# Tail tokens of two batches in one pass of the channel layers, with new work orders, in an attention and MLP-mixer kernel

## The chip, the cores and the metric

The kernel runs on one core of a Trainium2 chip. The metric is the device time of one execution in microseconds, as a median over several executions. Details come from one execution that was taken with the hardware profiler. All times are in microseconds (us) unless marked ns.

## The reference

What is computed is sliding-window attention with a distance bias for 8 batches, 8 heads, 576 tokens and head dimension 64, and then one mixer layer on its output x (576 tokens x 512 channels for each batch).

```python
scores = scale * np.matmul(q, k.transpose(0, 1, 3, 2))
rel = pos[:, None] - pos[None, :]
bias = slopes[:, None, None] * (-np.abs(rel))[None]
mask = (rel >= 0) & (rel < 128)
attn = softmax(np.where(mask, scores + bias[None], -1e9))
x = (attn @ v) with heads side by side          # 8 x 576 x 512

h = np.maximum(x^T @ w_tok1, 0.0) @ w_tok2      # over tokens: 576 -> 256 -> 576
u = x + h^T
h2 = np.maximum(u @ w_ch1, 0.0) @ w_ch2         # over channels: 512 -> 1536 -> 512
return u + h2
```

## The kernel before

The matrices are held in bf16, sums in fp32. A batch has 576 tokens: four blocks of 128 and a tail of 64. Everything that works on blocks of 128 tokens has a part of its own for the tail.

The work of a batch is cut into named steps, and the order in which they are issued is written out by hand as lists of names. A name without a mark is the current batch b; one mark means b+1, two b+2, three b+3. PROLOGUE and FIRST cover batch 0 and the start, SECOND batch 1, PERIOD is run for b = 2 to 6, LAST is batch 7. Each engine executes its own instructions strictly in the order of the list. The steps that matter here:

- S..: scores of one key block and four heads, on TensorE into one of two double banks psS, then an exp on ScalarE and a mask multiply on VectorE. The mask multiply is issued one step later than its scores (MASK_LATER). These matmuls contract over 64 rows.
- P0 to P3, P4: the product with V, also into psS; VectorE divides by the row sum (L382, L383; for the tail L408, L413) and so frees psS.
- K0, K1: the first token layer. U0 to U3: the second token layer and the add of x, giving the tile ub. UT: the same for the 64 tail tokens, which gives the transposed tile utt directly (psT, copied by ScalarE, L474).
- X0 to X3: transposes of ub into utb, which the channel layer reads. For batches 3 to 7 (U_DMA) the step is a DMA transpose of two blocks, issued from SyncE; for batches 1 and 2 it is a TensorE transpose and a copy, on VectorE for the blocks in X_DVE and on ScalarE for others. Batch 0 has its own forms u0 to u3 and x0 to x3, by pairs of heads; for a u in U_ACT the residual goes in by identity matmuls and ScalarE copies the result, for others VectorE adds it (L667, L669).
- C0 to C11: the first channel layer, one step for each of 12 blocks of 128 hidden channels: four matmuls of 512 columns into one of three banks psM, then a relu on VectorE (for the blocks in DVE_RELU, L504) or on ScalarE (L507). The three psM banks go round among C, D, E, K, U and X.
- T0, T1: the first channel layer for the 64 tail tokens of one batch: six hidden blocks each, 24 matmuls of 64 columns into the one bank psT, then one relu of ScalarE of 384 columns (L516, L519).
- D00 to D32: the second channel layer for the four token blocks, each in three parts of four matmuls, with an add of ub on VectorE and an output DMA at the end (L549 to L555).
- E0 to E2: the second channel layer for the tail. The tails of batches b-1 and b (b odd) make one block of 128 tokens, so E exists for odd b alone. After its 12 matmuls four identity matmuls of 128 columns add the transposed utt (L575), ScalarE copies the sum out (L579), and two output DMAs follow (L581).
- Lq, Lk, v: loads from GpSimd's queue. Zq, Zk: DMA transposes of queries and keys from SyncE's queue (L213, L216), which also takes all output DMAs. The loads of the next keys wait until Zk has read the previous ones.

Of the kernel before, what the change touches and what calls it, by code (L numbers as in the profile page):

```python
# [11 lines left out]
ALU = mybir.AluOpType  # L12
# [4 lines left out]
CH2_PARTS = 3  # L17
MASK_LATER = 1
U_DMA = (3, 4, 5, 6, 7)
U_ACT = (0, 1, 3)  # L20
X_DVE = (0, 1, 2)
K_DVE = (0,)
PROLOGUE = """
l0 I W2 q0 q1 J M3 l1 ck0 M0 W3 M1 W3 W3 l23 cq0 O qt m0 A0 q23 W3 v3 v0 ck1 v1 M2 FC W1 cq1 A1
# [1 line left out]
l23' A1' e1 qt' W2 v4' ek p2 u0 A0' p3 G1 k2 S00' LC G2 u1 v1'  # L26
"""
FIRST = """
H1 v3' k3 u2 v2' x0 u3 A3' v0' W1 H0 A2' Lk'' UT x2 x1 AT' Lq'' S20' x3 Zq'' Zk'' Lk''' T0 S10'
S01' v3'' v0'' Lq''' C9 v0''' S21' C11 v4'' C3 e2 S31' C0 C5 S30' C7 C8 S11' C10 E0 C1 C2 v2''  # L30
C4 P2' v4''' C6 P3' D00 P0' P4' T1 E2 v1'' P1' D01 D02 K0' K1' D10 U1' v2''' D11 D12 U2' UT'
Zq''' X1' U0' U3' D20 D30 S11'' S20'' v1''' D21 D31 E1 Zk''' S00'' D22 S01'' D32
"""
SECOND = """
T1 X2 X0 X3 S30' S31' T0 C8 C9 C7 C11 C2 P0' C5 Lk''' C3 v0''' C4 v1''' C1 S21' S10' C10 Lq'''
v2''' v3'' C0 P4' C6 D00 P3' D01 v3''' P1' P2' D02 K0' S20'' K1' v4''' S01'' D10 D11 D12 U1' U0'
UT' U2' U3' X0' S21'' S11'' D20 D21 X3' S10'' S00'' E0 E1 D22 E2 X2' D30 D31 X1' D32 P0''
# [12 lines left out]
SPLIT = (1, 2)  # L50
S_M = (0, 2, 4, 5, 6)
S_P = ()
x_DVE = (1, 2, 3)
k_DVE = (2,)
AK_DVE = (2, 3, 7)
AQ_ACT = (1, 3, 4, 5, 7)
DVE_RELU = (2, 3, 4, 5, 7, 8, 10, 11)


@with_exitstack  # L60
def kernel(
# [11 lines left out]
    nc = tc.nc  # L73
    P = nc.NUM_PARTITIONS
# [8 lines left out]
    ST = S - SM  # L83
    NHP = H // 2
    NHT = DCH // P
    NCB = DM // P
# [15 lines left out]
    psT = PS("psT", [P, 512])  # L102
# [15 lines left out]
    ident = T("ident", [P, P])  # L118
# [36 lines left out]
    utt = [T(f"utt{i}", [P, NCB, 2, ST]) for i in range(2)]  # L155
    r2 = [T(f"r2_{i}", [P, NHT, SM]) for i in range(2)]
    r2t = [T(f"r2t{i}", [P, NHT, 2, ST]) for i in range(2)]
    ob = [T(f"ob{i}", [P, DM], f32) for i in range(4)]
    orot = [0]

# [128 lines left out]
    def score(b, kb, j):  # L289
# [188 lines left out]
    def utrans(b, c):  # L478
# [9 lines left out]
        def f():  # L488
            t = M()[:, 0:256].bitcast(bf16)
            for cb in range(NCB):  # L490
                nc.tensor.transpose(t[:, cb * P:(cb + 1) * P],  # L491
                                    ub[b % 2][:, c, cb * P:(cb + 1) * P], ident[:, :])
            cp = nc.vector.tensor_copy if c in X_DVE else nc.scalar.copy
            cp(out=utb[b % 2][:, c, :, :], in_=t.rearrange("p (g x) -> p g x", g=NCB))
        return f

    def ch1(b, ht):
        def f():
            t = M()
            for cb in range(NCB):  # L500
                nc.tensor.matmul(t[:, :], lhsT=WC1[:, cb, ht * P:(ht + 1) * P],  # L501
                                 rhs=utb[b % 2][:, :, cb, :], start=(cb == 0), stop=(cb == NCB - 1))
            if ht in DVE_RELU:
                nc.vector.tensor_scalar(out=r2[b % 2][:, ht, :], in0=t[:, :], scalar1=0.0,  # L504
                                        scalar2=None, op0=ALU.max)
            else:
                nc.scalar.activation(out=r2[b % 2][:, ht, :], in_=t[:, :], func=ACT.Relu)  # L507
        return f

    def ch1_tail(b, g, n=6):  # L510
        def f():
            for j in range(n):
                ht = g * n + j
                o = psT[:, j * ST:(j + 1) * ST]
                for cb in range(NCB):
                    nc.tensor.matmul(o, lhsT=WC1[:, cb, ht * P:(ht + 1) * P],  # L516
                                     rhs=utt[(b // 2) % 2][:, cb, b % 2, :],
                                     start=(cb == 0), stop=(cb == NCB - 1))
# [40 lines left out]
    def ch2_tail(b, parts=2):  # L559

        st = {}
        pi2 = (b // 2) % 2

        def part(pi):
            def f():
                if pi == 0:
                    st["t"] = M()
                t = st["t"]
                n = NHT // parts
                for ht in range(pi * n, (pi + 1) * n):  # L570
                    nc.tensor.matmul(t[:, :], lhsT=r2t[pi2][:, ht, :, :], rhs=WC2[:, ht, :],  # L571
                                     start=(ht == 0), stop=False)
                if pi == parts - 1:
                    for cb in range(NCB):
                        nc.tensor.matmul(t[:, cb * P:(cb + 1) * P], lhsT=utt[pi2][:, cb, :, :],  # L575
                                         rhs=ident[:, :], start=False, stop=(cb == NCB - 1))
                    o = ob[orot[0] % len(ob)]
                    orot[0] += 1
                    nc.scalar.copy(out=o[:, :], in_=t[:, :])  # L579
                    for i in range(2):  # L580
                        nc.sync.dma_start(out=out[b - 1 + i, SM:S, :], in_=o[i * ST:(i + 1) * ST, :])  # L581
            return f
        return [part(i) for i in range(parts)]
# [183 lines left out]
    def names(b):  # L767

        d = {}
# [11 lines left out]
        d["UT"] = tok2_tail(b)  # L781
        for ht in range(NHT):
            d[f"C{ht}"] = ch1(b, ht)
        for g in range(2):
            d[f"T{g}"] = ch1_tail(b, g)
        for c in range(NC):
            for i, f in enumerate(ch2(b, c, CH2_PARTS)):
                d[f"D{c}{i}"] = f
# [49 lines left out]
        return d  # L838

    work = {b: names(b) for b in range(B)}  # L840

    def emit(order, b=0):
# [42 lines left out]
```

The softmax here doesn't subtract the row's maximum and nothing guards it: scores larger than these inputs give would overflow.

## Time and profile before

| What | Value |
|---|---|
| Median of six runs | 290.77 us (289.65 to 292.39) |
| The profiled execution | 292.39 us, of which the span of the profile is 290.7 us |
| Mean granted TensorE clock | 0.988 of full speed |
| Channel layer 1, blocks (L501) | 384 matmuls of 512 columns, 90.2 us busy |
| Channel layer 2, blocks (L549) | 372 matmuls of 512 columns, 86.5 us busy |
| Channel layer 1, tails (L516) | 384 matmuls of 64 columns, 13.8 us busy |
| Identity matmuls of the tails' residual (L575) | 16 of 128 columns, 1.5 us busy |
| VectorE relus (L504) / ScalarE relus (L507) | 64 of 686 ns / 32 of 597 ns |
| Token transposes by DMA (L481) | 10, median 6.3 us from issue to landing |
| Periods b = 2, 3, 4, 5, 6 in the chain | 30.84, 33.75, 30.95, 33.75, 29.08 us |

The busy time of a matmul in this table includes the time it takes to pass through the array, and matmuls overlap in it; their spacing is shorter and is seen in the order of starts. The periods are measured from the first channel matmul of one batch to the first of the next. Odd periods hold the E steps, even ones do not.

### The profile page before, as it was taken

Reading aid. Unit: us, or ns where it says so; the run is one execution under the profiler, and the core shown is the slowest. Engines: PE = TensorE matmul, PEld = TensorE weight load, DVE = VectorE, ACT = ScalarE, POOL = GpSimd, SP = SyncE. Lnnn points to the kernel's source line nnn. Section 1 sums busy time; section 2 is a strip of 40 time slices with the busy share of each in tenths; the row PEclk is TensorE's granted clock in tenths of the full one; section 3 lists DMA queues with packets and bytes.
Section 4 is the critical chain, followed back from the end, with each engine's and each line's share of the span. In section 5 each row is a group of like instructions: output and inputs, shape, how many; then the busy total and the mean of one; then the engine's idle time right before and its main releaser. Section 6 shows DMA issues by size and latency. Waiting matters only on the chain.

```text
span 290.7 us, 6456 instructions
## 1 busy us (share of the span) xinstructions
PE 281.0 (97%) x2707; PEld 155.1 (53%) x2707; DVE 177.3 (61%) x348; ACT 115.4 (40%) x176; POOL 99.6 (34%) x128
## 2 busy tenths in 40 slices
PE   7589999999999999999999999999999999999995
PEld 2347745646465556554665456644655456644543
DVE  3678778657777668456856467556846477426212
ACT  6678883137233631425332262435241263101300
POOL 8876543079409802940096003930000000000000
PEclk9779999999999999999999999999999999999999
DMA  6999999799999994999699975999703320051004
GB/s 167 163 198 193 199 185 141 143 166 143 144 192 130 176 214 94 131 160 186 145 104 162 134 183 95 130 161 185 142 2 86 97 72 2 36 111 72 2 36 144
DMA packets 148636, 38.00 MB, mean 131 GB/s; under 512 B 135808, under 2 KB 144128, under 8 KB 148608
## 3 DMA queue, kind: packets, MB, share of 16 engines
q0 software_dynamic: 103152, 17.41, 78.4%
q1 hardware_dynamic: 45456, 20.19, 31.6%
q8 instruction: 21, 0.34, 0.5%
q14 instruction: 7, 0.06, 0.1%
HBM read 35.85 MB, written 9.44 MB: 156 GB/s over the span
## 4 chain that ended last, share of the span: by engine, by line
PE 92%; DMA 2%; ACT 2%; POOL 1%; DVE 1%; issue 1%; POOLq 0%; DVEq 0%
PE psM L501 29%; PE psM L549 28%; PE psS L308 4%; PE psM L434 4%; PE psM L459 4%; PE psT L516 4%; PE psM L571 4%; PE psS L373 2%; DMA qs<-in_q_dram 2%; PE psS L369 2%; PE psS L401 1%; PE psS L312 1%; PE psM L229 1%; PE psM L530 1%; PE psM L491 1%; PE psT L687 1%
## 5 line engine op out<-in xcount | busy, mean ns | idle before, releaser
L501 PE MATMUL psM<-utb,WC 128*128 128x512 bf16 x384 | 90.2, 379 | 0.0
L549 PE MATMUL psM<-WC,r 128*128 128x512 bf16 x372 | 86.5, 379 | 0.0
L322 ACT ACTIVATE pe<-psS 128x1024 bf16<-128x1024 f32 (+1 forms) x60 | 58.5, 1010 | 51.6 <-PE psS L308 44.4
L549 PEld LDWEIGHTS <-r 128*128 128x128 bf16 x372 | 34.5, 98 | 40.7 <-issue 3.2
L501 PEld LDWEIGHTS <-WC 128*128 128x128 bf16 x384 | 34.6, 98 | 37.7 <-issue 1.9
L504 DVE TENSOR_SCALAR r<-psM 128x512 bf16<-128x512 f32 x64 | 43.3, 686 | 15.0 <-PE psM L501 14.5
L185 POOL DMA_DIRECT2D kn<-in_k_dram x24 | 21.0, 890 | 82.0 <-DMA kT<-kn 76.2
L329 DVE TENSOR_TENSOR pb<-pe,masks 128x1024 bf16<-128x1024 bf16 (+1 forms) x52 | 32.9, 638 | 23.1 <-ACT pe L322 22.0
L554 DVE TENSOR_TENSOR ob<-psM,ub 128x512 f32<-128x512 f32 x31 | 21.4, 691 | 32.1 <-PE psM L549 31.9
L507 ACT ACTIVATE r<-psM 128x512 bf16<-128x512 f32 x32 | 19.1, 597 | 54.4 <-PE psM L501 53.8
L185 POOL DMA_DIRECT2D vp<-in_v_dram x32 | 29.1, 954 | 2.2 <-DMA WC<-in_moe_w_ch_dram 1.5
L185 POOL DMA_DIRECT2D qn<-in_q_dram x24 | 21.3, 935 | 3.4 <-DMA WC<-in_moe_w_ch_dram 3.3
L383 DVE TENSOR_TENSOR xb<-psS,rt 128x512 bf16<-128x512 f32 x28 | 19.4, 691 | 1.0
L461 DVE TENSOR_TENSOR ub<-psM,xb 128x512 bf16<-128x512 f32 x28 | 18.0, 684 | 2.1 <-PE psM L459 1.8
L373 PE MATMUL psS<-vp,pb 128*128 128x65 bf16 x224 | 15.7, 193 | 0.0
L373 PEld LDWEIGHTS <-pb 128*128 128x128 bf16 x224 | 13.6, 97 | 3.3
L459 PE MATMUL psM<-r,W 128*128 128x512 bf16 x56 | 15.4, 379 | 0.0
L308 PE MATMUL psS<-qT,kT 64*128 64x256 bf16 x172 | 14.8, 275 | 0.3 <-ACT kT L234 0.3
L516 PEld LDWEIGHTS <-WC 128*128 128x128 bf16 x384 | 13.2, 98 | 3.1
L519 ACT ACTIVATE r2t<-psT 128x384 bf16<-128x384 f32 x16 | 7.9, 492 | 17.4 <-PE psT L516 16.8
L516 PE MATMUL psT<-utt,WC 128*128 128x64 bf16 x384 | 13.8, 193 | 0.0
L434 PE MATMUL psM<-xb,W 128*128 128x256 bf16 x112 | 13.4, 273 | 0.0
(125 smaller groups left out, 292.3 us busy)
## 6 DMA issues: line engine op xcount, KB each, us to landing
out_dram<-ob SPq DMA_DIRECT2D x31, 256.0 KB, 2.3
vp<-in_v_dram POOLq DMA_DIRECT2D x32, 128.0 KB, 6.3
kn<-in_k_dram POOLq DMA_DIRECT2D x24, 128.0 KB, 4.3
qn<-in_q_dram POOLq DMA_DIRECT2D x24, 128.0 KB, 4.9
WC<-in_moe_w_ch_dram POOLq DMA_DIRECT2D x3, 512.0 KB, 9.2
WC<-in_moe_w_ch_dram POOLq DMA_DIRECT2D x2, 768.0 KB, 14.4
out_dram<-ob SPq DMA_DIRECT2D x10, 128.0 KB, 2.3
ks<-in_k_dram POOLq DMA_DIRECT2D x3, 256.0 KB, 6.9
```

Of the source, the lines that this page charges most:

```text
L185: nc.gpsimd.dma_start(out=dst, in_=src[b, :, c * P:(c + 1) * P, :].rearrange("h s d -> s h d"))
L308: nc.tensor.matmul(s[h][:, a * 256:(a + 1) * 256], lhsT=kT[i][r, kb, hp, :], rhs=qT[i][r, kb:kb + 2, hp, :], start=True, stop=True)
L322: nc.scalar.activation(out=e[:, h, :], in_=s[n][:, None, :] if split else t2[:, :, :], func=ACT.Exp, scale=scale)
L329: nc.vector.tensor_tensor(out=p[:, :].rearrange("p (h x) -> p h x", h=2)[:, h], in0=e[:, h, :], in1=masks[:, j, h].rearrange("p h g a x -> ...
L373: nc.tensor.matmul(ov, lhsT=prob(b, qb, h, 0), rhs=vt[:, qb, h, 0:D + 1], start=first, stop=(hh == 3))
L434: nc.tensor.matmul(st["t"][h][:, dh * 256:(dh + 1) * 256], lhsT=W1[:, c, dh * P:(dh + 1) * P], rhs=by_half(xb[b % 2][:, c, :])[:, h], star ...
L459: nc.tensor.matmul(t[:, :], lhsT=W2[:, j, c * P:(c + 1) * P], rhs=r1[b % 2][:, j, :], start=(j == 0), stop=(j == 1))
L501: nc.tensor.matmul(t[:, :], lhsT=WC1[:, cb, ht * P:(ht + 1) * P], rhs=utb[b % 2][:, :, cb, :], start=(cb == 0), stop=(cb == NCB - 1))
L504: nc.vector.tensor_scalar(out=r2[b % 2][:, ht, :], in0=t[:, :], scalar1=0.0, scalar2=None, op0=ALU.max)
L516: nc.tensor.matmul(o, lhsT=WC1[:, cb, ht * P:(ht + 1) * P], rhs=utt[(b // 2) % 2][:, cb, b % 2, :], start=(cb == 0), stop=(cb == NCB - 1))
L549: nc.tensor.matmul(t[:, :], lhsT=r2[b % 2][:, ht, c * P:(c + 1) * P], rhs=WC2[:, ht, :], start=(ht == 0), stop=(ht == NHT - 1))
L554: nc.vector.tensor_tensor(out=o[:, :], in0=t[:, :], in1=ub[b % 2][:, c, :], op=ALU.add)
```

## The change

1. The tail step T exists for odd batches alone and then treats the tails of b-1 and b together: three groups T0, T1, T2 of four hidden blocks, each with 16 matmuls of 128 columns that fill the whole bank psT, and one relu of 512 columns.
2. For b in Y_DMA = (3, 5, 7) the residual of the tails is no longer added by identity matmuls. A new step Y transposes utt by DMA into a new tile ut2, and VectorE adds it to the sum as it is copied out. For b = 1 the four identity matmuls and ScalarE's copy stay.
3. Lists of engines: U_ACT loses pair 3, X_DVE is now block 3 alone (it was blocks 0, 1 and 2), DVE_RELU gains hidden block 1.
4. In FIRST the steps T0 and T1 of batch 0 are dropped with nothing put in their place. SECOND, PERIOD and LAST have new orders. PROLOGUE is the same.

```diff
-U_ACT = (0, 1, 3)
-X_DVE = (0, 1, 2)
+U_ACT = (0, 1)
+X_DVE = (3,)
 FIRST = """
-H1 v3' k3 u2 v2' x0 u3 A3' v0' W1 H0 A2' Lk'' UT x2 x1 AT' Lq'' S20' x3 Zq'' Zk'' Lk''' T0 S10'
+H1 v3' k3 u2 v2' x0 u3 A3' v0' W1 H0 A2' Lk'' UT x2 x1 AT' Lq'' S20' x3 Zq'' Zk'' Lk''' S10'
 S01' v3'' v0'' Lq''' C9 v0''' S21' C11 v4'' C3 e2 S31' C0 C5 S30' C7 C8 S11' C10 E0 C1 C2 v2''
-C4 P2' v4''' C6 P3' D00 P0' P4' T1 E2 v1'' P1' D01 D02 K0' K1' D10 U1' v2''' D11 D12 U2' UT'
-Zq''' X1' U0' U3' D20 D30 S11'' S20'' v1''' D21 D31 E1 Zk''' S00'' D22 S01'' D32
+C4 P2' v4''' C6 P3' D00 P0' P4' E2 v1'' P1' D01 D02 K0' K1' D10 U1' v2''' D11 D12 U2' UT' Zq'''
+X1' U0' U3' D20 D30 S11'' S20'' v1''' D21 D31 E1 Zk''' S00'' D22 S01'' D32
 """
 SECOND = """
-T1 X2 X0 X3 S30' S31' T0 C8 C9 C7 C11 C2 P0' C5 Lk''' C3 v0''' C4 v1''' C1 S21' S10' C10 Lq'''
-v2''' v3'' C0 P4' C6 D00 P3' D01 v3''' P1' P2' D02 K0' S20'' K1' v4''' S01'' D10 D11 D12 U1' U0'
-UT' U2' U3' X0' S21'' S11'' D20 D21 X3' S10'' S00'' E0 E1 D22 E2 X2' D30 D31 X1' D32 P0''
+X2 X0 X3 S30' S31' C3 C11 C2 C5 T0 Lk''' C7 v2''' C8 T1 P0' C9 C4 v0''' C1 S21' S10' C10 v1'''
+Lq''' C0 v3'' C6 P4' D00 P3' T2 P1' D01 v4''' P2' v3''' D02 K0' S01'' S11'' K1' D10 D11 D12 U0'
+U1' UT' U3' X0' S10'' S00'' U2' D20 X3' D21 S21'' S20'' D22 E0 E1 X2' E2 D30 D31 X1' D32 P0''
 """
 PERIOD = """
-C3 C7 Zq'' S31' S30' C10 C1 Zk'' C8 P1' C6 T1 P2' C11 P4' C2 C4 P3' C9 Lk''' v4''' C0 C5 K0'
-S00'' K1' S01'' D00 v0''' D01 D02 U2' T0 Lq''' v1''' U1' U0' UT' U3' P0'' D20 X3' v2''' X2'
-v3''' X0' D10 X1' D21 D22 S11'' S10'' D11 D30 D31 E0 D12 D32 E1 E2 S21'' S20''
+T0 Zq'' C0 C7 C2 S31' S30' C10 C1 C3 P2' T1 C5 T2 Zk'' C6 P3' C8 Lk''' v1''' C4 C9 P1' C11 P4'
+K0' Y K1' S00'' v0''' S01'' D00 D01 Lq''' D02 U2' U1' v2''' v4''' UT' X1' U3' X3' P0'' U0' X2'
+D20 X0' D10 D11 v3''' D21 D22 D30 S11'' S10'' D31 E0 D12 D32 S21'' S20'' E1 E2
 """
 LAST = """
-C8 C0 C3 C4 C7 C11 T1 C10 C9 T0 C6 C2 C1 C5 D00 E0 D01 D02 D10 D11 E1 D20 D12 E2 D21 D30 D31 D22
-D32
+C5 C9 C1 T2 C11 C0 C10 C7 T0 C8 C6 T1 C3 C2 C4 D00 E0 D01 D02 D10 E1 D20 D21 Y E2 D11 D12 D22
+D30 D31 D32
 """
+Y_DMA = (3, 5, 7)
-DVE_RELU = (2, 3, 4, 5, 7, 8, 10, 11)
+DVE_RELU = (1, 2, 3, 4, 5, 7, 8, 10, 11)
...
-    def ch1_tail(b, g, n=6):
+    def ch1_tail(b, g, n=4):
+        pi2 = (b // 2) % 2
         def f():
             for j in range(n):
                 ht = g * n + j
-                o = psT[:, j * ST:(j + 1) * ST]
                 for cb in range(NCB):
-                    nc.tensor.matmul(o, lhsT=WC1[:, cb, ht * P:(ht + 1) * P],
-                                     rhs=utt[(b // 2) % 2][:, cb, b % 2, :],
-                                     start=(cb == 0), stop=(cb == NCB - 1))
-            nc.scalar.activation(out=r2t[(b // 2) % 2][:, g * n:(g + 1) * n, b % 2, :],
-                                 in_=psT[:, 0:n * ST].rearrange("p (j x) -> p j x", j=n),
+                    nc.tensor.matmul(psT[:, j * P:(j + 1) * P], lhsT=WC1[:, cb, ht * P:(ht + 1) * P],
+                                     rhs=utt[pi2][:, cb, :, :],
+                                     start=(j == 0 and cb == 0), stop=(j == n - 1 and cb == NCB - 1))
+            nc.scalar.activation(out=r2t[pi2][:, g * n:(g + 1) * n, :, :],
+                                 in_=psT[:, :].rearrange("p (j i x) -> p j i x", j=n, i=2),
                                  func=ACT.Relu)
+    def utail_trans(b):
+        pi2 = (b // 2) % 2
+        def f():
+            nc.sync.dma_start_transpose(
+                out=ut2[pi2][:, :, :], in_=utt[pi2][:, :, :, :].rearrange("p c i x -> p (c i x)"))
+        return f
...
                 if pi == parts - 1:
-                    for cb in range(NCB):
-                        nc.tensor.matmul(t[:, cb * P:(cb + 1) * P], lhsT=utt[pi2][:, cb, :, :],
-                                         rhs=ident[:, :], start=False, stop=(cb == NCB - 1))
                     o = ob[orot[0] % len(ob)]
                     orot[0] += 1
-                    nc.scalar.copy(out=o[:, :], in_=t[:, :])
+                    if b in Y_DMA:
+                        nc.vector.tensor_tensor(out=o[:, :], in0=t[:, :],
+                                                in1=ut2[pi2][:, :, :].rearrange("p c x -> p (c x)"),
+                                                op=ALU.add)
+                    else:
+                        for cb in range(NCB):
+                            nc.tensor.matmul(t[:, cb * P:(cb + 1) * P], lhsT=utt[pi2][:, cb, :, :],
+                                             rhs=ident[:, :], start=False, stop=(cb == NCB - 1))
+                        nc.scalar.copy(out=o[:, :], in_=t[:, :])
```

More of the change, by code (lines that the diff above doesn't have):

```diff
@@ L157 @@
     r2t = [T(f"r2t{i}", [P, NHT, 2, ST]) for i in range(2)]
+    ut2 = [T(f"ut2_{i}", [P, NCB, P]) for i in range(2)]
     ob = [T(f"ob{i}", [P, DM], f32) for i in range(4)]
@@ L571, in f @@
                     nc.tensor.matmul(t[:, :], lhsT=r2t[pi2][:, ht, :, :], rhs=WC2[:, ht, :],
-                                     start=(ht == 0), stop=False)
+                                     start=(ht == 0), stop=(ht == NHT - 1 and b in Y_DMA))
                 if pi == parts - 1:
-                    for cb in range(NCB):
-                        nc.tensor.matmul(t[:, cb * P:(cb + 1) * P], lhsT=utt[pi2][:, cb, :, :],
-                                         rhs=ident[:, :], start=False, stop=(cb == NCB - 1))
                     o = ob[orot[0] % len(ob)]
                     orot[0] += 1
-                    nc.scalar.copy(out=o[:, :], in_=t[:, :])
+                    if b in Y_DMA:
[7 more added lines that the diff above has]
+                        nc.scalar.copy(out=o[:, :], in_=t[:, :])
                     for i in range(2):
@@ L783, in names @@
             d[f"C{ht}"] = ch1(b, ht)
-        for g in range(2):
-            d[f"T{g}"] = ch1_tail(b, g)
+        if b % 2:
+            for g in range(3):
+                d[f"T{g}"] = ch1_tail(b, g)
+            if b in Y_DMA:
+                d["Y"] = utail_trans(b)
         for c in range(NC):
```

## The prediction

> **What bounds the kernel now.** I read the page's busy shares first, then its chain of work that ended last, then that chain in order of time, and last the timeline of single engines at the places that the edit touches.
>
> ```profile
> PE 281.0 (97%) x2707; PEld 155.1 (53%) x2707; DVE 177.3 (61%) x348; ACT 115.4 (40%) x176; POOL 99.6 (34%) x128
> PE 92%; DMA 2%; ACT 2%; POOL 1%; DVE 1%; issue 1%; POOLq 0%; DVEq 0%
> ```
>
> TensorE is busy for 97% of the span and makes 92% of the chain. From the first channel layer at 36.07 us to 287.5 us no piece of the chain belongs to anything else. So after 36 us a matmul taken out is worth its streaming time, and another engine matters only where TensorE catches up with it. The chain in order of time shows the places where matmuls leave:
>
> ```profile
> 34.50 0.33 PE psM L676 x4
> 34.83 0.70 PE psT L516 x24
> 35.53 0.54 PE psS L308 x8
> 36.07 0.97 PE psM L501 x4
> ...
> 50.41 0.54 PE psS L401 x8
> 50.95 0.70 PE psT L516 x24
> 52.13 1.73 PE psM L549 x8
> ...
> 67.78 0.70 PE psT L516 x24
> 68.48 0.67 PE psM L491 x12
> 69.71 0.81 PE psT L516 x24
> 70.52 4.43 PE psM L501 x20
> ```
>
> Columns: start, length, what. L516 is a tail group of the first channel layer, 24 matmuls of 64 columns in 0.70 us. The chain is whole, so each group stands between two pieces without a gap; the reader should ask what the other engines do meanwhile. The timelines of ScalarE, of VectorE and of the DMA queue of SyncE answer:
>
> ```profile
> 34.54 1.02 ACT L322 ACTIVATE pe<-psS 128x1024 bf16<-128x1024 f32 x1
> ```
>
> ```profile
> 50.69 0.69 DVE L383 TENSOR_TENSOR xb<-psS,rt 128x512 bf16<-128x512 f32 x1
> ...
> 67.82 0.69 DVE L554 TENSOR_TENSOR ob<-psM,ub 128x512 f32<-128x512 f32 x1
> ...
> 69.03 0.74 DVE L494 COPY utb<-psM 128x512 bf16<-128x512 bf16 x2
> ```
>
> ```profile
> 168.88 1.12 SPq L581 DMA_DIRECT2D out_dram<-ob  x2
> 170.23 1.47 SPq L213 DMA_TRANSPOSE qT<-qn  x1
> ...
> 191.27 4.80 SPq L481 DMA_TRANSPOSE utb<-ub  x2
> ```
>
> These are evacuations that now end under a tail group, and the output, head transposes and token transposes of one period, in queue order.
>
> **What the Trainium skill says.** "TensorE: Matmul & The Clock Gate", section "Back-to-back issue gap", gives N/2.4 + 2.5 ns for N columns: 29.2 ns for 64, 55.8 for 128. The trace agrees: 0.70 us / 24 = 29.2 ns, and twelve transposes of 128 columns (L491) take 0.67 us, 55.8 each. (It also says 81 ns for streams with a weight load each; this trace doesn't.) "DMA: Bandwidth & Descriptors", section "Issuing engines are not separate DMA queues", says that DMAs of all engines share 16 DMA engines and interleave. The trace agrees: the token transposes land 6.1 to 7.0 us after issue while loads run (126 to 193 us), and 3.2 to 3.6 us when none do (222 to 258 us). "VectorE: DVE Perf Modes", section on the TRN2 errata, gives (N+151)/0.96 ns for an fp32 add: 691 ns for 512; L554 has mean 691.
>
> **Part by part.**
>
> *Tails of two batches together.* Before: 8 batches x 2 groups x 0.70 = 11.2 us. After: 4 pairs x 3 groups x 16 matmuls of 128 columns = 192 x 55.8 ns = 10.7. The columns stay the same; only the fixed cost of half the instructions goes: -0.5 us. ScalarE's relus become 12 of 512 columns (0.60 each, as L507) for 16 of 0.49; it is 40% busy, so nothing.
>
> *Residual.* In three of four pairs four identity matmuls go: 12 x 55.8 ns = -0.67 us. The output add moves from ScalarE (L579, 0.59) to VectorE (0.69). The DMA transpose that feeds it reads tiles finished a period earlier; it stands behind kT's transposes in SyncE's queue, some 10 us before anything else of that queue is due. The nearest rows, kT's and qT's tails (64 x 512), hold the queue 1.2 to 1.4 us and land after 2.3 to 4 us. Its reader comes over 15 us later, except for the last pair: there it is issued about 1.2 us after D02 ends and read 4.3 us after, and the bank has 1.7 us to spare. Cost 0, up to 0.5 if cover is gone.
>
> *u3 from ScalarE to VectorE (U_ACT).* Four matmuls go, 0.22 us. Around 31 to 33.5 us the chain runs through evacuations: an idle of 0.45 us, a copy of kT at 32.23 and one of qT (0.69) that frees a bank for the transposes at 33.57. VectorE stands idle 1.23 us before the first, so u3's add (0.68) fits; the pair can start up to 0.5 us earlier. Bounds 0 and -0.5; I take -0.35.
>
> *X_DVE, DVE_RELU.* Eight relus and three outputs go to VectorE, four transposes' copies leave it: + 8 x 0.69 + 3 x 0.69 - 4 x 0.42 = +5.9 us on an engine busy for 177. In the channel phase of an even period it then has about 11.5 us of work in some 13. Between queued instructions the trace shows a pitch of 0.60 us for 0.69 long, so I count 0, and 0.3 us per even period at worst.
>
> *First batch: two groups gone with nothing in their place.* Batch 0's groups now run with batch 1's. T0 stood at 34.83. Without it S10' follows at once, but S01' needs the score bank of S20', whose exp ends at 34.54 + 1.02 = 35.56; with 0.05 us for the handover it starts at 35.61, where it started at 35.85 before. Saved 0.24 of 0.70: a stall of 0.46. T1 stood at 50.95. Without it P1' needs the bank of P0', which the multiply of 50.69 frees at 51.38; start 51.43, 0.48 late.
>
> *Start of the second batch.* Before, T1 and T0 stood around the transposes (0.70 + 0.81 = 1.51 us). Now X3 needs the bank of D32, freed at 67.82 + 0.69 = 68.51; its copy comes behind a mask on VectorE, 69.03 to 69.45, and the first channel matmul can start at 69.50 instead of 70.52: 1.02 saved, 0.49 lost.
>
> *Periods.* Groups of 64-row score matmuls, each with about 0.1 us on entry and exit (1.83 for 1.73), count 82 changes in either order. Walking banks and queues of the new PERIOD and LAST with rows of the page, I find no wait over 0.1 us but one: the token transposes. An even period has no tail groups any more: 30.95 - 1.40 = 29.5 us, and T0 (0.89) opens the next one, so the first channel matmul comes 30.4 us after the period's start where it was 30.95. In batch 4 the transposes were issued at 191.3 and 192.6 and landed 6.1 to 6.5 us later, by 198.7 to 199.1, against a start at 199.72: slack 0.6 to 1.0. The slack loses 0.5, and 1.2 more: E2 ends the odd period and its add waits on VectorE for the last mask, so the outputs that stood at 168.88 come that much later against the period's start, and behind them on SyncE the head transposes, hence the loads that wait for kT. The transposes themselves are issued about 1.5 us earlier, but finish with the loads. A wait of 0 to 0.9 us before batch 5; I take 0.4. Batch 3 has slack 0.1 to 0.7 and loses 0.5: 0 to 0.4, taken as 0.
>
> **Sum.** -0.5 - 0.67 - 0.35 = -1.52; + 0.46 + 0.48 + 0.49 + 0.4 = +1.83; net +0.3 us. Durations are of the execution of 292.39 us, whose span is 290.7 (1.7 around it); the six runs have median 290.77. The difference carries over: 291.1 us.
>
> **Rivals.**
>
> *All waits are filled:* the stalls at the three places without tail groups are shorter than counted, because the earlier steps shift too, and the transposes land in time. For: VectorE and ScalarE are 61% and 40% busy. Against: each stall is the end of a named instruction. 290.77 - 1.52 = 289.2 us.
>
> *Token transposes land late (slower):* at the first channel matmul of batches 3 and 5. If their landing moves with the loads in full, batch 5 waits 31.6 - 30.4 = 1.2 us (landing 199.1 - 168.77 = 30.3, plus 1.2, rounded up) and batch 3 0.4; with the stalls, -1.52 + 1.43 + 1.6 = +1.5, or 292.3 us. It decides from 1.5 us of such waits on. For: 6 us landings beside loads. Against: the transposes are issued earlier and get a share.
>
> *VectorE becomes the bound in the even channel phases:* 0.3 us in three periods, 292.0 us with the rest; it adds to the former rather than stands alone.
>
> That the edit is no edit is excluded: TensorE has 208 matmuls fewer in the built program (192 + 12 + 4).
>
> **How the numbers follow.** Likeliest case (291.1) 0.47; filled waits 0.21; late transposes, with VectorE's queue as its companion, 0.32. The range runs from the filled case with the full 0.5 us at u3 (289.1, less 0.2 of noise: 288.9) to the late case with VectorE's 0.6 more (292.9, rounded to 293.0); the likeliest case's own range is 290.0 to 292.0. One measurement can't tell less than 0.5% (1.45 us) from no change, so faster means under 289.3 and slower over 292.2. That gives 0.21, 0.47 and 0.32.
>
> **What would show it.** L516 as 192 matmuls, 16 in 0.89 us; L575 down to 4. Stalls before S01' and P1' and at X3 and the first L501 of batch 1, each near 0.5 us, with ACT or DVE as releaser in the chain. From one even period's start to the next channel matmul 30.4 us if the token transposes are in time; a DMA piece utb<-ub in the chain if not. I am wrong if the chain names none of these, if a piece of DVE stands in the channel phases, or if the ut2 transpose is in the chain at all.

## The result, and the profile after

| | Before | Changed | Ratio, 95% interval |
|---|---|---|---|
| First series: median (lowest to highest, executions) | 290.93 us (289.65 to 292.39, 41) | 293.15 us (290.11 to 298.86, 20) | 1.0056 [1.0037, 1.0075] |
| Second series, other executions of the same kernel | 290.56 us (61) | 293.24 us (291.73 to 295.34, 14) | 1.0083 [1.0059, 1.0108] |
| Profiled execution | 292.39 us, span 290.7 | 292.01 us, span 290.3 | |

The change makes the kernel slower, by 0.4 to 1.1% over both series. The ratio of the first series leaves out six executions of 296 us or more as disturbed, two of them at the ordinary mean clock of 0.993, so it is smaller than the quotient of the medians and may be too small. The changed kernel also scatters more. In the second series, executions at a mean granted clock of 0.991 to 0.996 take 291.7 to 295.3 us (11 of them, median 293.3), those of before 290.4 to 292.1 (29, median 290.9).

The two spans can't be compared as they stand. In the profiled execution of before, TensorE was granted half its clock for 6.8 us near the start, in that of the changed kernel for 3.4, and before reached the first scores of batch 1 (L308) 1.6 us later. From there to the end it takes 290.69 - 28.04 = 262.65 us, the changed kernel 290.30 - 26.43 = 263.87: 1.2 us more.

The busy shares and the chain by engine on the page after:

```profile
PE 279.6 (96%) x2499; PEld 153.3 (53%) x2499; DVE 182.7 (63%) x356; ACT 110.0 (38%) x164; POOL 99.7 (34%) x128
PE 85%; DMA 5%; DVE 3%; ACT 3%; POOL 1%; issue 1%; SPq 0%; POOLq 0%; ACTq 0%
```

TensorE has the 208 matmuls fewer that it should have, and its share of the chain falls from 92 to 85%. So what was saved in matmuls is spent in waiting. The chain in order of time (start, length, what; "..." stands for lines left out) shows where:

```profile
32.42 0.37 ACT kT L259
32.79 0.99 ACT pe L324
33.83 0.39 PE psS L310 x4
...
47.40 0.87 PE psM L562 x4
...
48.79 0.70 DVE xb L385
...
50.18 1.73 PE psM L562 x8
...
64.57 0.69 DVE ob L567
65.26 0.60 DVE pb L331
65.86 0.70 DVE ob L567
66.61 0.38 PE psM L493 x4
...
67.55 3.62 PE psM L503 x16
...
189.66 0.69 DVE ub L463
...
190.73 8.27 DMA utb<-ub
199.13 2.75 PE psM L503 x12
```

At four places another engine's work stands in the chain where it was all TensorE before: an exp at 32.79, a multiply by the row sum at 48.79, an add and a mask from 64.57 on, and a token transpose by DMA at 190.73. The first three are the places where the tail groups stood. The view of TensorE's waits (us in total, times, longest) gives their sizes:

```profile
PE psS L371 <- DVE xb L385: 0.5, 1, 0.5
PE psM L503 <- DMA utb<-ub: 0.5, 1, 0.5
PE psS L310 <- ACT pe L324: 0.5, 1, 0.5
PE psM L493 <- DVE ob L567: 0.3, 1, 0.3
```

SyncE's queue in the period of batch 4, which starts at 168.06 us:

```profile
169.57 1.13 SPq L599 DMA_DIRECT2D out_dram<-ob  x2
170.92 1.75 SPq L215 DMA_TRANSPOSE qT<-qn  x1
...
174.03 2.56 SPq L215 DMA_TRANSPOSE kT<-kn  x1
...
188.93 4.41 SPq L483 DMA_TRANSPOSE utb<-ub  x2
```

The head transposes start 2.9 us after the period does (1.5 before), and the token transposes 20.9 us after it (22.6 before). They land 7.4 and 8.3 us after their issue, where it was 6.5 and 6.1, and the first channel matmul of batch 5 (L503) waits for the second of them.

Stretch by stretch, from the starts of the records in both profiles. The wait for transposes is what the period of batch 4 has above 30.44 us, the length of the period of batch 2.

| Stretch | Before | Changed | Difference | Foretold |
|---|---|---|---|---|
| exp after the first scores to exp of S20' (L322, L324) | 6.06 | 5.88 | -0.18 | -0.35 |
| exp of S20' to D10 | 21.33 | 21.16 | -0.17 | -0.46 |
| D10 to the first channel matmul of batch 1 | 14.48 | 13.63 | -0.85 | -1.02 |
| batch 1, with three tail groups more | 33.67 | 36.17 | +2.50 | +2.67 |
| batches 2 and 3 | 64.69 | 64.36 | -0.33 | -0.35 |
| batches 4 and 5, without the wait | 64.70 | 64.35 | -0.35 | -0.35 |
| the wait before batch 5 | 0 | 0.63 | +0.63 | +0.4 |
| batches 6 and 7, to the issue of the last output | 54.60 | 54.29 | -0.31 | -0.35 |
| from there to the end of the span | 2.69 | 2.96 | +0.27 | 0 |

The sum is +1.21. (A matmul's record starts up to 0.17 us early while the array is busy, and this falls between the third and the fourth row; the chain has -1.01 and +2.66 for them. "Foretold" for rows five, six and eight is two tail groups of 0.70 twice against three of 0.89, -0.13, and four matmuls of 55.8 ns, -0.22.) In this profile no row is off by more than 0.3 us, but nearly all err on the same side, and together they turn the +0.2 foretold into +1.2. The row that isn't the same in every execution is the wait.

### The profile page after: what moved, and what is told of

Same layout as the page of the kernel before. It is cut to its first block, busy times and chain, and to the rows that moved or that the text cites. A ratio compares the mean times of both kernels' runs of the same rounds, so it can differ in the third digit from the quotient of the medians.

```text
span 290.3 us, 6038 instructions
## 1 busy us (share of the span) xinstructions
PE 279.6 (96%) x2499; PEld 153.3 (53%) x2499; DVE 182.7 (63%) x356; ACT 110.0 (38%) x164; POOL 99.7 (34%) x128
## 4 chain that ended last, share of the span: by engine, by line
PE 85%; DMA 5%; DVE 3%; ACT 3%; POOL 1%; issue 1%; SPq 0%; POOLq 0%; ACTq 0%
PE psM L503 29%; PE psM L562 25%; PE psM L436 4%; PE psM L584 4%; PE psM L461 4%; PE psS L310 3%; PE psT L520 3%; DMA utb<-ub 3%; PE psS L375 2%; DMA qs<-in_q_dram 2%; PE psS L371 2%; ACT pe L324 1%; PE psS L403 1%; PE psS L314 1%; PE psM L231 1%
## 5 line engine op out<-in xcount | busy, mean ns | idle before, releaser
L503 PE MATMUL psM<-utb,WC 128*128 128x512 bf16 x384 | 89.7, 379 | 0.5 <-DMA utb<-ub 0.5
L324 ACT ACTIVATE pe<-psS 128x1024 bf16<-128x1024 f32 (+1 forms) x60 | 57.8, 1008 | 52.3 <-PE psS L310 43.5
L506 DVE TENSOR_SCALAR r<-psM 128x512 bf16<-128x512 f32 x72 | 48.8, 687 | 13.8 <-PE psM L503 13.5
L503 PEld LDWEIGHTS <-WC 128*128 128x128 bf16 x384 | 35.0, 98 | 38.3 <-issue 1.5
L509 ACT ACTIVATE r<-psM 128x512 bf16<-128x512 f32 x24 | 14.4, 599 | 42.9 <-PE psM L503 42.8
L375 PE MATMUL psS<-vp,pb 128*128 128x65 bf16 x224 | 15.9, 193 | 0.0
L310 PE MATMUL psS<-qT,kT 64*128 64x256 bf16 x172 | 14.1, 275 | 0.7 <-ACT pe L324 0.5
L523 ACT ACTIVATE r2t<-psT 128x512 bf16<-128x512 f32 x12 | 7.2, 598 | 17.4 <-PE psT L520 17.4
L371 PE MATMUL psS<-vp,pb 128*128 128x65 bf16 x168 | 13.0, 193 | 0.5 <-DVE xb L385 0.5
L310 PEld LDWEIGHTS <-kT 64*128 64x128 bf16 x188 | 7.3, 94 | 11.0 <-issue 8.9
(126 smaller groups left out, 293.3 us busy)
```

Source lines behind the costliest of these rows:

```text
L310: nc.tensor.matmul(s[h][:, a * 256:(a + 1) * 256], lhsT=kT[i][r, kb, hp, :], rhs=qT[i][r, kb:kb + 2, hp, :], start=True, stop=True)
L324: nc.scalar.activation(out=e[:, h, :], in_=s[n][:, None, :] if split else t2[:, :, :], func=ACT.Exp, scale=scale)
L375: nc.tensor.matmul(ov, lhsT=prob(b, qb, h, 0), rhs=vt[:, qb, h, 0:D + 1], start=first, stop=(hh == 3))
```

## The experiments

*Again.* The changed kernel a second time, for its scatter.

> The changed kernel once more, for its spread and a second profile. If the wait for the token transposes before batch 5 (0.5 us in the first profile, 190.73 + 8.27 in its chain) is a race between the transposes and the loads, it differs from run to run: the same three stalls of about 0.5 us at the first batches, 1.2 to 1.4 us together, and a wait of anything from 0 to several us before the first channel matmul of batch 3 or 5. If the run times spread for another reason, the period lengths of this profile are those of the first within 0.2 us.

Measured: the ratio of the second series above. In its profile (span 291.7) the three stalls in the first two batches are the same to 0.03 us, but the token transposes land after 8.8 and 9.1 us, and the period of batch 4 takes 32.19 us, so the wait is 1.75 where it was 0.63. The view of waits names another engine here:

```profile
PE psM L503 <- DVE pb L331: 1.6, 1, 1.6
```

This mask ends at 200.48 us and the second transpose lands at 200.39, 0.13 us before the matmul starts. In the first profile the same matmul starts 1.1 us before the same mask ends, and again 0.13 us after the landing, so it waits for the transpose and not for the mask. Between these two profiles the wait is the part of the time that changes.

*Fills at the three places.* A step of other work is put where a tail group stood.

```diff
-S01' v3'' v0'' Lq''' C9 v0''' S21'
+v3'' v0'' Lq''' C9 S01' v0''' S21'
...
-P0' P4' E2 v1'' P1' D01 D02
+P0' P4' E2 v1'' D01 P1' D02
...
-X2 X0 X3 S30' S31' C3 C11 C2 C5 T0 Lk'''
+T0 X2 X0 X3 S30' S31' C3 C11 C2 C5 Lk'''
```

> The three places where tail groups left are filled: C9 goes before S01', D01 before P1', and T0 of the first pair to the start of the second batch. Theory of the hand-off stalls: 0.4 + 0.4 + 0.5 = 1.1 to 1.4 us less than the changed kernel, with the spread of its runs kept. Rival, that the loss lies in the periods (VectorE's extra relus and the late token transposes): under 0.4 us less.

Measured: 292.11 us, ratio 1.0058 [1.0036, 1.0079]. The two fills in FIRST take 0.38 and 0.48 us out of their stretches. The third gains nothing, as the chain shows:

```profile
66.10 0.91 PE psT L520 x16
...
67.52 1.08 ACT utb L496 x2
68.64 5.48 PE psM L503 x24
```

T0 now covers VectorE's add, but ScalarE has T0's relu and then two copies of transposes, and the first channel matmul waits for these. The stall has moved to another engine. The changed kernel has 1.0083 in the same series, so the fills bring about 0.7 us, as the two in FIRST should; but the intervals overlap, and the time alone doesn't decide. The profiled execution is the slowest of this run (295.62 us, mean clock 0.983). In it the token transposes land after 8.6 and 10.2 us and cost 2.2 us.

*E1 and E2 ahead of two scores in PERIOD*, so that the tail's add doesn't stand behind their masks on VectorE and the outputs and head transposes come earlier.

```diff
-E0 D12 D32 S21'' S20'' E1 E2
+E0 D12 D32 E1 E2 S21'' S20''
```

> In the period, E1 and E2 go back before S21'' and S20'', as the kernel before has them; all else as changed. Theory of the late token transposes: the outputs of E2 and the head transposes behind them start about 1.2 us earlier after an odd period, the loads with them, the wait before batch 5 is gone (0.5 us or more) and the run times spread less; 0.5 to 2 us less than the changed kernel in the median. Rival (VectorE's load, or the ut2 transpose): no change within 0.3 us and the same spread.

Measured: 292.93 us, ratio 1.0073 [1.0046, 1.01], against 1.0083 for the changed kernel in the same series: a miss. SyncE's queue in the profile of this kernel, whose period starts at 169.04:

```profile
170.68 1.76 SPq L215 DMA_TRANSPOSE qT<-qn  x1
172.54 1.20 SPq L218 DMA_TRANSPOSE qT<-qnt  x1
173.79 3.72 SPq L215 DMA_TRANSPOSE kT<-kn  x1
```

The queries' transpose does come 1.2 us earlier in its period. But the keys' transpose holds the queue for 3.72 us instead of 2.56, the next loads of keys start no earlier (11.2 us into the period, 11.1 in the changed kernel), the token transposes land after 9.0 and 9.1 us, and the wait is 1.63. What makes the keys' transpose slow there stays open.

*The residual by identity matmuls again.*

```diff
-Y_DMA = (3, 5, 7)
+Y_DMA = ()
```

> The residual goes back to identity matmuls and ScalarE's copy for all pairs; no ut2 transpose, order as changed. By matmuls alone: 12 x 55.8 ns = 0.67 us more than the changed kernel. Theory of the late token transposes: E2's output leaves about 0.7 us earlier after odd periods, so part of the wait before batch 5 goes: between 0.67 more and 0.5 less, and less spread. If the ut2 transpose itself disturbs the loads, well below the changed kernel: 1 us less or more.

Measured: 291.87 us, ratio 1.0048 [1.0027, 1.0069]. Odd periods are 0.22 us longer, as four matmuls of 55.8 ns should make them. Yet the kernel is some 1.0 us faster than the changed one in the same series (1.0083), where the matmuls alone would make it 0.67 slower; the intervals just overlap. The outputs of E2 leave 0.8 us into the period of batch 4, where it was 1.5 with VectorE's add, the loads of keys start at 9.95 us into it instead of 11.06, the transposes land after 7.4 and 7.2 us, and in this profile there is no wait. This fits the loads' start bearing on the landing, which the run before couldn't move. It is one profile, of one of this run's faster executions (291.07 us), so it doesn't show it.

*Two groups of the pair in the even period.* The pair's utt is complete long before the even period ends, so two of its groups can go there. That delays the first channel matmul of the odd batch by two groups and leaves the transposes where they are.

```diff
-T0 Zq'' C0 C7 C2 S31' S30' C10 C1 C3 P2' T1 C5 T2 Zk'' C6
+T2 Zq'' C0 C7 C2 S31' S30' C10 C1 C3 P2' C5 Zk'' C6
...
-D20 X0' D10 D11 v3''' D21 D22 D30 S11''
+D20 X0' D10 T0' D11 v3''' D21 D22 T1' D30 S11''
...
-C5 C9 C1 T2 C11 C0 C10 C7 T0 C8 C6 T1 C3
+C5 C9 C1 T2 C11 C0 C10 C7 C8 C6 C3
```

> As the changed kernel, but the tail groups T0 and T1 of an odd batch are issued between the second channel layer's parts of the even batch before it (after D10 and after D22), and T2 alone opens the odd period. TensorE's work is the same; the first channel matmul of batches 3, 5 and 7 comes 1.8 us later after the token transposes are issued. Theory of the late token transposes: no wait before batch 5 is left (0.6 to 2.2 us in the profiles so far), the median is 1 to 2 us under the changed kernel's and the runs spread less. Rival (VectorE, or hand-offs inside the periods): no change within 0.4 us.

Measured: 291.32 us (290.3 to 292.94), ratio 1.0015 [0.9992, 1.0038]. The chain around the start of batch 5:

```profile
190.91 0.89 PE psT L520 x16
...
194.40 0.89 PE psT L520 x16
...
199.93 1.00 PE psT L520 x16
200.93 2.59 PE psM L503 x12
```

The transposes land even later, 8.6 and 9.6 us after issue, and nobody waits: the two groups fill the time. The wide scatter is gone with the wait.

*Without the loads beside the transposes* of the period of batch 4:

```diff
-d[f"v{c}"] = lambda c=c: load_v(b, c)
+d[f"v{c}"] = lambda c=c: load_v(b, c) if b < B - 1 else None
```

> As the changed kernel, but the loads of V of batch 7, which stand in batch 4's period beside the token transposes of batch 5, are left out (the output of batch 7 is computed with old V). Nothing else moves. If the transposes land late because of the loads beside them, they land 3 to 5 us after issue instead of 7 to 9, the wait before batch 5 is gone, and the time is 0.6 to 2 us under the changed kernel's. If they are late by themselves (queue order on SyncE, issue), the wait stays.

Measured: 291.13 us (290.11 to 291.92), ratio 1.0009 [0.9993, 1.0025]. The two token transposes of that period, and the chain behind them:

```profile
L483 SPq DMA_TRANSPOSE utb<-ub x2: 1261/2036/2812, 187.9 to 190.9; - x2
DMA to landing us min/median/max: 3.2/4.3/5.4
```

```profile
196.14 0.54 PE psS L310 x8
196.68 1.00 PE psT L520 x16
197.68 2.59 PE psM L503 x12
```

Without the five loads of V the transposes land after 5.4 and 3.2 us and the wait is gone. So the loads beside them are what makes them late.

*Pairing alone, on the kernel before.* Its lists and U_ACT, X_DVE, DVE_RELU and identity matmuls stay; T becomes three groups of 128 columns for odd batches and none for even ones, with T2 put in by hand.

```diff
-    def ch1_tail(b, g, n=6):
+    def ch1_tail(b, g, n=4):
...
-        for g in range(2):
-            d[f"T{g}"] = ch1_tail(b, g)
+        if b % 2:
+            for g in range(3):
+                d[f"T{g}"] = ch1_tail(b, g)
...
-C2 P0' C5 Lk'''
+C2 P0' C5 T2 Lk'''
...
-P4' C2 C4 P3' C9 Lk'''
+P4' C2 T2 C4 P3' C9 Lk'''
...
-C9 T0 C6 C2 C1 C5 D00
+C9 T0 C6 C2 T2 C1 C5 D00
```

> The kernel before with one part of the change: the tails of two batches together (three groups, odd batches), at the old places T1 and T0 with T2 in the channel phase; old orders, old lists, residual by identity matmuls. By matmuls -0.5, by the two empty places in the first batch up to +0.9, so +0.4 us. Theory of the late token transposes: an even period has no tail group before its end and none opens the odd one, so the first channel matmul of batches 3 and 5 comes 1.4 us earlier against loads that haven't moved: waits of 0.5 to 1 us at each, +1.4 to +2.4 us in all. Rival, that it takes the new lists or the ut2 transpose to lose time: +0.4 us and no wait.

Measured: 292.45 us, ratio 1.0056 [1.0038, 1.0075], as for the whole change in its first series. TensorE's waits:

```profile
PE psM L501 <- DMA utb<-ub: 0.9, 1, 0.9
PE psS L369 <- DVE xb L383: 0.5, 1, 0.5
PE psS L308 <- ACT pe L322: 0.5, 1, 0.5
```

So the loss needs neither the new orders nor the new lists nor the transposed residual. Taking the tail groups out of batch 0 and of the even periods makes both kinds of wait. That the ratio is the same is chance: pairing alone saves 0.9 us of matmuls less, but it has neither the stall at the start of the second batch nor, as is shown below, the longer end.

*All repairs together:* two groups in the even period, the two fills in FIRST as above, and T0 further on in SECOND.

```diff
-X2 X0 X3 S30' S31' C3 C11 C2 C5 T0 Lk'''
+X2 X0 X3 S30' S31' T0 C3 C11 C2 C5 Lk'''
```

> The early tail groups of the run before, with C9 before S01' and D01 before P1' in the first batch, and T0 between S31' and C3 in the second. Sum of the theory against the kernel before: matmuls -1.2, start of the second batch and S01', P1' together about +0.5 instead of +1.4, no wait for transposes: 0.5 to 1.2 us less than the kernel before. If the periods hide another loss, no better than the kernel before.

Measured: 290.74 us, ratio 1.0000 [0.998, 1.0021]. The profile shows no wait for transposes and none of the two stalls in FIRST; 0.3 us at L493 for VectorE's add are left.

*u3 back on ScalarE*, in the last version.

```diff
-U_ACT = (0, 1)
+U_ACT = (0, 1, 3)
```

> The version that came out best so far (290.74 us) with u3 of batch 0 back on ScalarE (U_ACT = (0, 1, 3): four identity matmuls and a copy on ScalarE, as in the kernel before). The prediction took 0.35 us for this part; the traces of before and after differ by 0.15 in the stretch from the first scores L308 to the exp of S20'. Theory: this stretch grows by 0.1 to 0.2 us and the time by as much, which its interval can't show. Rival, the prediction's own figure: the stretch grows by 0.35 to 0.5 us.

Measured: 290.52 us, ratio 0.9997 [0.9982, 1.0013], no difference from the version without the edit. From exp to exp the stretch is 6.34 us here. It is 5.88 us, to 0.01, in every profile with u3 on VectorE, and 6.06 and 6.07 in the two kernels with the old lists. VectorE's record in this kernel says where the time stands:

```profile
31.71 0.69 DVE L236 COPY kT<-psM 128x512 bf16<-128x512 bf16 x1 [1.21 <-ACT qT L236]
```

As in the kernel before, VectorE idles 1.2 us for TensorE and ScalarE; with u3 on VectorE this gap takes the add. The old and the new order are the same up to S20', so the order doesn't make 6.34 out of 6.06. What differs is VectorE's place at the start: its last multiply by the row sum of batch 0 stands 0.63 us before the first exp in this profile, and 0.96 and 0.95 us in those of before and of pairing alone. From that multiply to the exp of S20' it is 6.97 us here and 7.02 there. So 0.18 us is the fairer figure for the part; the other 0.28 of the 0.46 fits a VectorE that comes 0.3 us late, in one profile.

*T0 first in SECOND again, now with the copies split* (block 0 to VectorE), on the version with all repairs.

```diff
-X_DVE = (3,)
+X_DVE = (0, 3)
...
-X2 X0 X3 S30' S31' T0 C3 C11 C2 C5 Lk'''
+T0 X2 X0 X3 S30' S31' C3 C11 C2 C5 Lk'''
```

> The changed kernel with two tail groups of each pair in the even period and the two fills in FIRST, as in the run before (290.74 us, ratio 1.000), but with T0 in front of the transposes at the start of SECOND, and with the copies of the transposes split: blocks 0 and 3 on VectorE, 1 and 2 on ScalarE. Theory: the group fills the 0.5 us in which X3 waits for VectorE's add of D32, and it failed alone only because ScalarE then had its relu and two copies in a row (1.08 us for the copies); with one copy less on ScalarE, the stretch from D10 of batch 0 to the first channel matmul of batch 1, which holds one group of 0.89 us, is 14.1 to 14.3 us (14.58 before), and the time 290.3 to 290.5. Rival: the copies wait for ScalarE's relu or for VectorE's masks and adds anyway; the stretch stays at 14.5 to 14.7 and the time at 290.7.

Measured: 290.63 us, ratio 0.9998 [0.9983, 1.0013]; the chain:

```profile
65.48 0.89 PE psT L520 x16
66.38 0.46 PE psM L493 x8
66.86 0.77 DVE utb L496 x2
67.67 5.37 PE psM L503 x24
```

The stretch from D10 falls from 14.58 to 14.03 us: with one copy less on ScalarE the fill that failed alone works. The time doesn't show it. In this profile, of the run's slowest execution (292.01 us), batch 1 waits 0.5 us for a load of V and batch 5 again 0.3 for a transpose that landed after 10.1 us.

*One output DMA for two tails* of the pairs in Y_DMA, on that version. Here the end of the span is at issue. SyncE closes the program by waiting for each of its semaphores in turn. The starts of these waits in the trace's event records, with a bar where the wait for the last output holds them up:

```
before   288.38 288.44 288.50 288.57 288.63 288.69 288.98 | 289.74 289.80                             end 290.69
changed  287.72 287.79 | 289.05 289.12 289.18 289.24 289.30 289.36 289.42                             end 290.30
```

In both the last output (issued at 288.00 and 287.34) is there after 1.7 us, but in the changed kernel five waits more stand behind it, 0.06 us each. The records also show why: SyncE's DMAs take eight semaphores in turn, and the last output is SyncE's 79th DMA before and its 82nd in the changed kernel.

```diff
-for i in range(2):
-    nc.sync.dma_start(out=out[b - 1 + i, SM:S, :], in_=o[i * ST:(i + 1) * ST, :])
+nc.sync.dma_start(out=out[b - 1:b + 1, SM:S, :], in_=o[:, :])
```

> The version before (two tail groups of each pair in the even period, the fills in FIRST and SECOND, copies split; 290.63 us) with one output DMA of 256 KB instead of two of 128 KB for the tails of batches 2 and 3, 4 and 5, 6 and 7. In the traces the time from the start of the last output DMA to the end of the span is 2.68 to 2.70 us in the three kernels without the residual's DMA transposes and 2.96 to 3.00 in the nine with them, though the last output itself lands after 1.7 us in both: SyncE then goes through its closing waits one after the other, 0.06 us each, and in the kernels with the transposes seven of them stand behind the one for the last output, where two stand behind it in the kernels without. Theory: which wait the last output gets goes round with the number of DMAs on SyncE's queue; the three transposes turned it by three, three output DMAs fewer turn it back, and the stretch is 2.7 us. Rival: the stretch belongs to the transposes themselves and stays at 2.96 to 3.00. Beside this the head transposes of an odd period come some 0.6 us earlier, as one issue of the two goes; the wait for the token transposes in the period of batch 4, 0.2 us in the profile of the version before, should be gone. The time should be 290.1 to 290.5 us, 0.3 under the version before, within what its interval can tell.

Measured: 294.13 us, ratio 1.0113 [1.0083, 1.0142], a bad miss on the time, though the stretch from the last output to the end is 2.68 us, as the theory has it (79 DMAs). SyncE's queue shows why, in the period of batch 4 and at the end:

```profile
168.09 7.09 SPq L215 DMA_TRANSPOSE qT<-qn  x1
...
280.22 0.55 SPq L599 DMA_DIRECT2D out_dram<-ob  x1
281.95 1.20 SPq L568 DMA_DIRECT2D out_dram<-ob  x2
283.85 5.02 SPq L549 DMA_DIRECT2D out_dram<-ob  x2
```

The one DMA takes 7.75 us in the chain, where 256 KB of a token block land in 2.4; the last add (L547) stands idle 4.27 us for it, and the queries' transpose behind another such DMA holds the queue for 7.09. The Trainium skill, "DMA: Bandwidth & Descriptors", section "Why a DMA increments its semaphore by 16 and not by 1", says that a copy runs on as many DMA engines as the largest number up to 16 that divides the slowest dimension (of a size above one) of both sides. Here that would be 2, the two batches. The trace agrees: in the DMA records some 24 packets of 2 KB start per us at the end of this transfer, 84 ns each, which is the work of 2.0 engines.

*The same turn with five DMAs more.* Five block outputs are cut in two instead, on the version with the copies split.

```diff
-nc.sync.dma_start(out=out[b, c * P:(c + 1) * P, :], in_=o[:, :])
+n = 2 if b == 6 or (b == 7 and c == 0) else 1
+for i in range(n):
+    h = slice(i * P // n, (i + 1) * P // n)
+    nc.sync.dma_start(out=out[b, c * P + h.start:c * P + h.stop, :], in_=o[h, :])
```

> The version with the split copies (290.63 us), with its tail outputs as in the changed kernel, and five block outputs of 256 KB (the four of batch 6 and the first of batch 7) sent as two DMAs of 128 KB each, of 64 tokens. Three output DMAs fewer brought the stretch from the last output's issue to the end of the span from 2.98 to 2.68 us, but the DMAs that did it, which put two batches' tails into one, took 7.75 us and cost more than they brought. Five DMAs more on SyncE's queue are the same turn if there are eight waits to go round. Theory: the stretch is 2.7 us again and the end comes 0.25 to 0.3 us earlier, with nothing else changed: the periods stay at 32.1 to 32.5, 29.4 for batch 6, and the time is 290.3 to 290.4, a change that the interval can't show. Rival: the turn isn't a count modulo eight, and the stretch stays at 2.98.

Measured: 290.32 us, ratio 0.9974 [0.9958, 0.999]. From the last output, here the 87th DMA, to the end it is 2.67 us, so the count goes round by eight. The periods of batches 2 to 5 are 32.22, 32.13, 32.22 and 32.13: no wait for transposes, though they land after 8.3 and 8.5 us. This is the only version below the kernel before by more than its interval, 0.7 us against the before of its own series. The turn explains 0.3 of it; stretch by stretch its profile is 1.0 us under that of before, and the split copies have a part in that.

## Why the prediction was wrong on the size, and where it was right

It took 291.1 us, no change, as likeliest. The ratio of the first series puts the changed kernel at 290.77 x 1.0056 = 292.4 us, that of the second at 293.2: slower by over 0.5% in both estimates (the first interval begins at 0.37%), which was the rival "token transposes land late" at 292.3 us. The whole range, up to 293.0, holds the first estimate and just misses the second. Its upper end counts 0.6 us of VectorE's queue, which cost nothing (the rival itself has 0.3 in each of three periods, 0.9), so that it came so near owes something to luck.

*The step that failed* is the wait for the token transposes, "I take 0.4". The place was right (batch 5, not batch 3), and so was what makes it: an even period without tail groups, 30.44 us against 30.4 foretold. The size was not one number. Two profiles of the changed kernel show 0.63 and 1.75 us, and two of versions near it 2.21 and 1.63; the landings in these four go from 7.4 to 10.2 us. In the first profile the wait makes only 0.2 of the 1.0 us by which the sum was short, FIRST and the end of the program 0.3 each; in the second it makes 1.35. The prediction carried over the 6.1 to 6.5 us of the one profile it had, added the shift of the loads and took the middle of 0 to 0.9. It also wrote "the transposes are issued earlier and get a share" as an argument against the late case, and that was the wrong way round: issued 1.7 us earlier, against loads that start 0.6 us later (11.1 us into the period, 10.5 before), they run beside these loads for longer. Both are slower there: the last load of V, issued 0.6 us later in the period, lands after 8.1 us where it took 6.6, and the second transpose lands 30.9 and 32.1 us into the period (30.0 before). That the loads do it is shown by the run without V of batch 7 (5.4 and 3.2 us, no wait), and that the wait carries most of the loss, and the scatter, by the run with two groups in the even period.

*Why the loads stand there* was only partly found. The outputs and head transposes do come 1.2 to 1.4 us later in the period, as foretold. But moving E1 and E2 forward brought no load forward, since the keys' transpose grew longer. Pairing alone, with the old place of E2, has 0.9 us of the wait as well, with landings of 6.7 and 7.2 us: there the first channel matmul simply comes sooner. How much of the wait in the changed kernel is owed to the late loads wasn't isolated; the run with the old residual only suggests that some of it is.

*Residual, -0.67.* The matmuls are worth what was foretold, 0.22 us in each odd period. "Cost 0" for the transposes holds on the path, and no record waits for ut2. But the add on VectorE delays E2's outputs and with them the loads, and three DMAs more on SyncE's queue turned the order of its closing waits and cost 0.27 us at the end. The run with five DMAs more shows that this is a matter of their number, not of transposes.

*u3, -0.35.* Measured 0.18, about half; the bounds 0 and -0.5 held. With u3 on VectorE the chain runs through two of its adds (28.64 and 29.84 us) before it comes to the copies, so one wait took the place of another.

*The stalls in FIRST.* The foretold net gain was 0.24 and 0.22 us; the trace has 0.17 for both together, so 1.23 of the 1.40 us of the two groups were lost. The same releasers as foretold stand there (an exp and a multiply), and each fill then took 0.4 to 0.5 us out. What makes the other 0.4 us of the loss stays open.

*Start of the second batch, 0.49 lost:* 0.50 in the chain, with the add, the mask and the add of VectorE in a row as described. Filling it needs ScalarE free as well, which the prediction didn't look at and the run with the fills showed.

*Tails, -0.5,* as foretold: 0.89 us for 16 matmuls, 55.8 ns each.

*Rivals.* No piece of VectorE is in a channel phase of the chain, so that one is out. "All waits are filled" at 289.2 us was not reached: the mended versions without the turn at the end come to 290.6 and 290.7. Not all was filled in them. Stretch by stretch, the profile of the version with all repairs is 0.2 us under that of before, where 1.5 was foretold: 0.5 us is still lost around the start of the second batch, 0.4 in FIRST and 0.3 at the end, and u3 is worth 0.2 less.

## What to carry to other kernels

A short group of matmuls on its own bank is cover for every hand-off around it: before it is taken out, look for what ends within its length on the other engines, and put some other step that needs neither in its place. A slack of a microsecond for a DMA transpose that runs beside loads is none: its landing moved by 0.8 and 1.5 us between two executions of one program, and by up to 3 us over these versions. So leave it more slack than that, or put work in front of the matmul that reads it. Where two kernels differ by half a per cent, the end of the program and the scatter of one transfer weigh as much as the edit.

## What the runs showed of the hardware

- A DMA transpose of two blocks lands 3.1 to 3.6 us after issue when no loads run, and 4.1 to 10.2 us beside them. Two executions of the same program have 7.4 and 8.3, and 8.8 and 9.1 us, for the same two transposes.
- An output of 256 KB whose destination has the two batches as its slowest dimension takes 7.75 us, against 2.4 for one of 128 tokens in one batch, and DMA transposes behind it on the same queue wait: 7.09 us in the queue for 1.77.
- The end of these programs depends on how many DMAs SyncE has issued, since its closing waits go through eight semaphores in a fixed order: from the last output to the end it is 2.67 to 2.70 us in the five profiles with 79 or 87 DMAs and 2.96 to 3.00 in the nine with 82.
- The start differs between executions of one program: TensorE is granted half its clock for 6.8 us in the profile of before, 3.4 in that of the changed kernel, and not at all in the one without the loads of V (mean clocks 0.988, 0.994 and 1.0). In the 61 executions of before in the second series the medians at about these mean clocks are 292.3, 290.9 and 290.0 us.
